# Row 4's x by the crossbar, chunk 2 and 3 re-stepped, and dilated v loaded without unread keys

## The chip, the core and the metric

The kernel runs on one core of a Trainium2 chip. The metric is the device time of one execution in microseconds. Three runs of the kernel before gave 302.06, 304.31 and 308.46 us, a median of 304.31 us.

The engines are named as the profile names them: PE (TensorE, with PEld for its weight loads), DVE (VectorE), ACT (ScalarE), POOL (GpSimd) and SP (SyncE, which here only issues DMAs). All transfers of the core go through 16 DMA engines.

## What is computed

Attention over 8 batch rows of 576 tokens and 8 heads of 64, followed by a feed-forward layer with squared ReLU on the 4608 tokens. Heads 0 to 3 use a sliding window of 32 keys, heads 4 to 7 a dilated window: 32 keys at a distance of 4.

```python
rel = pos[:, None] - pos[None, :]
mask_plain = (rel >= 0) & (rel < window)                                   # window = 32
mask_dil = (rel >= 0) & (rel < window * dilation) & (rel % dilation == 0)  # dilation = 4
attn = softmax(where(mask, q @ k.T / 8, -1e9))
x = (attn @ v), heads side by side        # (4608, 512)
h = x @ w_in                              # w_in (512, 2048)
out = relu(h) ** 2 @ w_out                # w_out (2048, 512), out (4608, 512) float32
```

## The kernel before

**Two loops laid over each other.** The attention works by batch row (0 to 7, 576 tokens each), the feed-forward layer by chunk (0 to 8, 512 tokens each). While PE does chunk c of the feed-forward layer, the attention of row c + 1 is woven in. The feed-forward work is a generator (`moe_gen` for chunks 1 and 2, `moe_seven_gen` from chunk 3 on) that yields every two to four matmuls. One yield is a step. `run` (L760) takes plans such as "34:d0 36:d1" and, at the step given, issues that part of the attention. The order of everything is thereby written out by hand: `PLANS` (L979) holds for each chunk the parts of its own row and of the row after.

**Parts of a row.** `z0`, `z1` are the dilated scores with exponential and mask (L619, L586, L590), `s0`, `s1` the sliding ones (L605). `d0`, `d1` are the products with the values for the first half of the dilated queries (tile t = 0), `e0`, `e1` for the second half (t = 1) (L680). `a0`, `a1`, `a2` are those of the sliding heads (L658). Each ends in `normalize` on DVE (L643, L644), which writes x in half precision with tokens on partitions. The feed-forward layer needs x transposed, in `xT`.

**Two ways to transpose x.** For rows under `CROSS` (5) the parts `x0`, `x1`, `y0`, `y1` do it on PE (L701, L719) with a copy by ACT (L707, L725). For rows from `CROSS` on, the `a`, `d` and `e` parts issue DMA transposes through the crossbar on SP's queue instead (L670, six per row; L689, four per row), and `w0`, `w1` (`place_dilated`, L732) put the dilated part in its place by ACT copies. Chunk c needs the first tokens of row c + 1 in `xT` when it starts.

**Accumulators.** Parts take pairs of PSUM banks in turn from a ring of two (`pair`), so that a part waits until the pair two before it has been read.

**Values.** v comes from HBM in float32 by SP's queue. `load_dilated_v` (L164) has two loads: for t = 0 72 keys (L169, 288 KB), for t = 1 128 keys (L167, 512 KB), each key with 4 heads of 1 KB. They go into `sd`, of which there is one. POOL casts `sd` to half precision (`cast_dilated_v`, L211) before `d` and `e` can run. `sd` can be loaded again when its casts are done. For the sliding heads `load_sliding_v` (L159) has six loads per row.

**SP's queue.** SP issues in the order of the program and waits in that order. In chunk 3 it goes: outputs of chunk 2 (L331), crossbar transposes of row 5's dilated k and q (L256), its sliding k and q to HBM (L244) and back through the crossbar (L252), row 5's `sd` (L169, L167), row 5's `sv` (L159), outputs of chunk 3 (L440). From chunk 4 on the ten crossbar transposes of x (L689, L670) stand between `sd` and `sv`: the code adds `load_sliding_v` for the next row at step 38 where the present row is at `CROSS` or above.

Of the kernel before, what the change touches and what calls it, by code (L numbers as in the profile page):

```python
# [13 lines left out]
P = 128  # L14
# [3 lines left out]
def kernel(  # L18
# [9 lines left out]
    nc = tc.nc  # L28

    B, H, S, D = q.shape  # L30
    W = 32
# [17 lines left out]
    CL = S // DIL  # L49
    QD = CL // 2  # L50
    PADD = P - QD
# [68 lines left out]
    sd = stg.tile([P, 2, HH, DIL * D], FP32, name="sd")  # L120
# [18 lines left out]
    def load_dilated_qk(b, m):  # L139
        for i, s in ((1, k), (0, q)):  # L140
            nc.gpsimd.dma_start(
                out=m[64 * i : 64 * (i + 1), :],
                in_=s[b, HH:H].rearrange("h (p j) d -> (h p) (j d)", j=36),
            )
# [19 lines left out]
    def load_dilated_v(b, t):  # L164
        vv = v[b, HH:H].rearrange("h (i c) d -> i h (c d)", c=DIL)
        if t:
            nc.sync.dma_start(out=sd[:, 1, :, :], in_=vv[QD - PADD : CL])  # L167
        else:
            nc.sync.dma_start(out=sd[PADD:P, 0, :, :], in_=vv[0:QD])  # L169

    def load_v(b, dilated_first=False):
        if not dilated_first:
            load_sliding_v(b)
        for t in range(2):
            load_dilated_v(b, t)
        if dilated_first:
            load_sliding_v(b)
# [350 lines left out]

    CROSS = 5

    def pt(wide):
        return pair(FP16)[:, 0, :] if wide else bank(FP16)
# [104 lines left out]
    def normalize(b, what, pav, w, n=2):  # L639
        x = xp.tile([QB, 2, HH, D], FP16, name=f"x{b}_{what}", tag="x")  # L640
        rcp = xp.tile([QB, 2, HH], FP32, name=f"rcp{b}_{what}", tag="rcp")
        pv = pav[0:w, 0:n, 0 : HH * (D + 2)].rearrange("p i (h d) -> p i h d", d=D + 2)
        nc.vector.reciprocal(rcp[0:w, 0:n], pv[:, :, :, D])  # L643
        nc.vector.tensor_tensor(  # L644
            out=x[0:w, 0:n],
            in0=pv[:, :, :, 0:D],
            in1=rcp[0:w, 0:n].unsqueeze(3).to_broadcast([w, n, HH, D]),
            op=ALU.mult,
        )
        return x  # L650

    def av_sliding(b, xs, *ms):

        pav = pair()
        for i, m in enumerate(ms):
            for h in range(HH):
                off = (h % 2) * 288 + (m % 3) * QB
                nc.tensor.matmul(  # L658
                    pav[:, i, h * (D + 2) : h * (D + 2) + D + 1],
                    AT[:, 2 * (h // 2) + m // 3, off : off + P],  # L660
                    vp[b % 2][:, m, h, 0 : D + 1],
                    start=True,
                    stop=True,
                )
        x = normalize(b, f"p{ms[0]}", pav, QB, len(ms))
        for i, m in enumerate(ms):
            if b < CROSS:
                xs[m] = x[:, i]
            else:
                nc.sync.dma_start_transpose(  # L670
                    out=xT[b % 3][:, 0:2, QB * m : QB * (m + 1)],
                    in_=x[:, i].rearrange("p h d -> p (h d)"),
                )

    def av_dilated(b, t, a):
        pav = pair()
        for e in range(2):
            for h in range(HH):
                off = e * 288 + h * QD
                nc.tensor.matmul(  # L680
                    pav[:, e, h * (D + 2) : h * (D + 2) + D + 1],
                    AT[:, 4 + 2 * a + t, off : off + P],
                    vd[b % 2][:, t, 2 * a + e, h, 0 : D + 1],
                    start=True,
                    stop=True,
                )
        x = normalize(b, f"d{t}_{a}", pav, QD if b < CROSS else QX)
        if b >= CROSS:
            nc.sync.dma_start_transpose(  # L689
                out=xd[:, t, 2 * a : 2 * a + 2].rearrange("p e c q -> p (e c) q"),  # L690
                in_=x[0:QX].rearrange("p e h d -> p (e h d)"),
            )
        return x

    def x_sliding(b, half, xs, wide):
        px = pt(wide)
        for m3 in range(3):
            m = 3 * half + m3
            x = xs[m].rearrange("p h d -> p (h d)")
            for c in range(2):  # L700
                nc.tensor.transpose(  # L701
                    px[:, 288 * c + QB * m3 : 288 * c + QB * (m3 + 1)],
                    x[:, P * c : P * (c + 1)],
                    ident[0:QB, 0:QB],
                )
        t0 = 288 * half
        nc.scalar.copy(  # L707
            xT[b % 3][:, 0:2, t0 : t0 + 288],
            px[:, 0:UW].rearrange("x (c t) -> x c t", c=2),
        )  # L710

    def x_dilated(b, t, xs, wide):
        py = pt(wide)
        for a in range(2):
            for e in range(2):
                x = xs[a][:, e].rearrange("p h d -> p (h d)")
                for c in range(2):
                    o = 288 * c + QD * (2 * a + e)
                    nc.tensor.transpose(  # L719
                        py[:, o : o + QD],  # L720
                        x[0:QD, P * c : P * (c + 1)],
                        ident[0:QD, 0:QD],
                    )
        t0 = 288 * t
        nc.scalar.copy(  # L725
            xT[b % 3][:, 2:4, t0 : t0 + 288].rearrange("x c (i r) -> x c i r", r=DIL),
            py[:, 0:UW].rearrange("x (c r i) -> x c i r", c=2, r=DIL),
        )
# [8 lines left out]
    def row_parts(b, wide):  # L737
# [9 lines left out]
            "a2": lambda: av_sliding(b, xs, 4, 5),  # L747
            "x0": lambda: b < CROSS and x_sliding(b, 0, xs, wide),
            "x1": lambda: b < CROSS and x_sliding(b, 1, xs, wide),
            "d0": lambda: ys.append(av_dilated(b, 0, 0)),  # L750
            "d1": lambda: ys.append(av_dilated(b, 0, 1)),
            "e0": lambda: zs.append(av_dilated(b, 1, 0)),
            "e1": lambda: zs.append(av_dilated(b, 1, 1)),
            "y0": lambda: b < CROSS and x_dilated(b, 0, ys, wide),
            "y1": lambda: b < CROSS and x_dilated(b, 1, zs, wide),
# [24 lines left out]
    reli = const.tile([P, QB], I16, name="reli")  # L780
    load_dilated_qk(0, nd0)
    nc.vector.memset(sd[0:64, 0, :, :], 0.0)
    nc.vector.memset(sv[0:PADP, 0, :, :], 0.0)
    nc.gpsimd.iota(reli, pattern=[[1, QB]], base=0, channel_multiplier=-1)
    make_identity(nc, ident)
    load_sliding_qk(0, ns0[0], 0)
    nc.gpsimd.memset(sd[64:65, 0, 0, 0:1], 0.0)
    load_sliding_qk(0, ns0[1], 1)
    load_dilated_v(0, 0)
    load_sliding_v(0, 0, 4)  # L790
    load_dilated_v(0, 1)
    load_sliding_v(0, 4, 6)

# [128 lines left out]
    for i, src in ((1, k), (0, q)):  # L922
        nc.gpsimd.dma_start(
            out=ns1[64 * i : 64 * (i + 1)],
            in_=src[1, 0:HH].rearrange("h (p j) d -> p h (j d)", j=9),
# [42 lines left out]
    for leaves in kept[:2]:  # L968
# [7 lines left out]
    SOON = "{}:z0 {}:z1 {}:s0 {}:s1"  # L976
    EARLY = "{}:d0 {}:d1 {}:e0 {}:y0 {}:e1 {}:a0 {}:y1 {}:a1 {}:a2 {}:x0 {}:x1"
# [1 line left out]
    PLANS = {  # L979
        1: (SOON.format(*range(24, 40, 4)) + " " + EARLY.format(*range(40, 62, 2)), ""),  # L980
        2: (
            SOON.format(18, 22, 26, 30) + " " + EARLY.format(34, 36, 38, 40, 41, 43, 45, 49, 51, 54, 59),
            SOON.format(49, 54, 60, 63),
        ),
        3: (
            EARLY.format(8, 11, 14, 17, 19, 22, 24, 27, 30, 33, 36),
            SOON.format(40, 45, 50, 55),
        ),
        4: (LATER[0] + " 57:w0 60:w1", LATER[1]),
        5: (LATER[0] + " 57:w0 60:w1", LATER[1]),  # L990
# [71 lines left out]
```

## Time and profile before

| | |
|---|---|
| three runs | 302.06, 304.31, 308.46 us, median 304.31 |
| the profiled execution | 300.74 us, span of its instructions 298.8 us |
| granted TensorE clock | 1.000 |
| PE busy | 289.2 us, 97% of the span |
| DVE, ACT, POOL busy | 203.7, 164.2, 67.6 us |
| DMA traffic | 84145 packets, 48.62 MB; HBM 189 GB/s over the span |
| SP's DMA queue (q1) | 76720 packets, 34.39 MB, 52.6% of 16 engines' span |
| POOL's DMA queue (q0) | 7248 packets, 13.63 MB, 26.0% |

Busy time is the time in which an engine had an instruction in work. The share of a DMA queue is the time that its packets took, summed over the 16 DMA engines and divided by 16 spans. SP itself has no busy time: its lines in a timeline are the stretches in which it was issuing a transfer. Such a line begins when SP reaches the instruction, and its length includes waiting for a semaphore or for room in the queue.

### The profile page before, as it was taken

The numbers are of one execution on the slowest core, as the hardware profiler recorded it, in microseconds if no ns is written. First come the engines' busy times: TensorE is split into PE (matmuls) and PEld (weight loads), VectorE is DVE, ScalarE is ACT, GpSimd is POOL, SyncE is SP. The second block draws the span as 40 slices with busy tenths as digits, with TensorE's granted clock in tenths as the row PEclk, the third lists the DMA queues.
The fourth block names the chain that finished last, engine by engine and source line by source line (L and its number), as shares of the span: only waits on it lengthen the run. The fifth ranks groups of instructions, "written<-read, shape, count | busy, mean of one in ns | idle before, by whom it ended". The sixth has DMA issues, their size and how long they took to land.

```text
span 298.8 us, 7670 instructions
## 1 busy us (share of the span) xinstructions
PE 289.2 (97%) x3152; PEld 218.5 (73%) x3152; DVE 203.7 (68%) x378; ACT 164.2 (55%) x280; POOL 67.6 (23%) x113
## 2 busy tenths in 40 slices
PE   3999999999999998999999999999999999999995
PEld 2779855555557755699889988998888876785584
DVE  7686645587723573389798979896979744853674
ACT  1768754778446954766435636563656326405610
POOL 5490017004505112620721350202230000000000
PEclk9999999999999999999999999999999999999999
DMA  6999999699999999998999998989274230022013
GB/s 115 236 209 214 211 218 223 141 186 238 172 288 199 230 208 162 236 257 189 222 241 241 166 201 81 245 186 190 40 207 99 64 107 0 2 70 70 2 35 105
DMA packets 84145, 48.62 MB, mean 163 GB/s; under 512 B 62672, under 2 KB 80336, under 8 KB 83920
## 3 DMA queue, kind: packets, MB, share of 16 engines
q1 hardware_dynamic: 76720, 34.39, 52.6%
q0 software_dynamic: 7248, 13.63, 26.0%
q8 instruction: 24, 0.39, 0.5%
q10 hardware_dynamic: 144, 0.13, 0.1%
q14 instruction: 9, 0.07, 0.1%
HBM read 39.85 MB, written 16.52 MB: 189 GB/s over the span
## 4 chain that ended last, share of the span: by engine, by line
PE 78%; DMA 13%; POOL 3%; DVE 2%; SPq 2%; issue 1%; ACT 0%; POOLq 0%; DVEq 0%
PE PS L266 37%; PE PS L410 24%; PE PS L307 10%; DMA nd<-in_k_dram 5%; DMA sd<-in_v_dram 3%; DMA n<-in_q_dram 3%; DMA sv<-in_v_dram 2%; PE PS L680 2%; PE PS L658 2%; PE PS L619 1%; SPq L159 1%; PE PS L605 1%; PE PS L719 1%; DVE S L396 1%; PE PS L701 1%
## 5 line engine op out<-in xcount | busy, mean ns | idle before, releaser
L266 PE MATMUL PS<-xT,wi 128*128 128x288 f16 (+8 forms) x1024 | 133.6, 286 | 0.0
L275 ACT ACTIVATE rt<-PS 128x512 f16<-128x512 f32 (+2 forms) x160 | 88.7, 555 | 62.0 <-PE PS L266 58.7
L266 PEld LDWEIGHTS <-wi 128*128 128x128 f16 x1024 | 97.4, 114 | 25.9
L300 DVE TENSOR_TENSOR g<-rt 128x1024 f16<-128x1024 f16 (+1 forms) x64 | 44.1, 690 | 33.2 <-ACT rt L275 33.0
L586 ACT ACTIVATE AT<-PS 128x576 f16<-128x576 f32 x64 | 38.5, 650 | 22.9 <-PE PS L605 14.7
L307 PE MATMUL PS<-wo,g 128*128 128x512 f16 x192 | 49.3, 379 | 0.0
L410 PEld LDWEIGHTS <-S 128*128 128x128 f16 x384 | 37.0, 98 | 4.6
L211 POOL CAST vd<-sd 128x512 f16<-128x512 f32 x32 | 25.0, 812 | 43.6 <-DMA sd<-in_v_dram 28.6
L410 PE MATMUL PS<-T,S 128*128 128x256 f16 x288 | 34.1, 273 | 0.0
L410 PEld LDWEIGHTS <-g 128*128 128x128 f16 x288 | 27.5, 98 | 4.0 <-issue 0.2
L207 POOL CAST vp<-sv 128x512 f16<-128x512 f32 x24 | 16.7, 702 | 55.4 <-DMA sv<-in_v_dram 53.2
L307 PEld LDWEIGHTS <-g 128*128 128x128 f16 x192 | 15.6, 98 | 12.6
L410 PE MATMUL PS<-wo,g 128*128 128x256 f16 x192 | 23.4, 273 | 0.0
L644 DVE TENSOR_TENSOR x_d<-PS,rcp_d 72x512 f16<-72x512 f32 (+1 forms) x32 | 22.0, 687 | 1.1
L590 DVE TENSOR_TENSOR AT<-AT,maskd 128x1152 f16<-128x1152 f16 x14 | 12.2, 873 | 14.2 <-ACT AT L586 14.1
L590 DVE TENSOR_TENSOR AT<-AT,maskp 128x1152 f16<-128x1152 f16 x14 | 11.0, 787 | 10.8 <-ACT AT L586 10.8
L644 DVE TENSOR_TENSOR x_p<-PS,rcp_p 96x512 f16<-96x512 f32 (+1 forms) x25 | 16.6, 665 | 0.9
L680 PEld LDWEIGHTS <-AT 128*128 128x128 f16 x256 | 11.9, 100 | 4.7 <-DVE x_d L644 1.1
L680 PE MATMUL PS<-vd,AT 128*128 128x65 f16 x256 | 13.8, 197 | 0.3 <-DVE x_d L644 0.2
L289 DVE TENSOR_TENSOR g<-rt 128x288 f16<-128x288 f16 x32 | 9.8, 307 | 5.5 <-ACT rt L275 5.3
L410 PE MATMUL PS<-T,g 128*128 128x256 f16 x96 | 12.0, 273 | 0.1
L410 PE MATMUL PS<-wo,S 128*128 128x256 f16 x96 | 11.5, 273 | 0.0
(89 smaller groups left out, 246.6 us busy)
## 6 DMA issues: line engine op xcount, KB each, us to landing
out_dram<-c SPq DMA_DIRECT2D x23, 256.0 KB, 2.2
sv<-in_v_dram SPq DMA_DIRECT2D x40, 128.0 KB, 5.7
sd<-in_v_dram SPq DMA_DIRECT2D x8, 512.0 KB, 6.1
dp<-o SPq DMA_DIRECT2D x12, 288.0 KB, 4.0
out_dram<-ot SPq DMA_DIRECT2D x11, 256.0 KB, 8.2
sd<-in_v_dram SPq DMA_DIRECT2D x8, 288.0 KB
wo<-in_moe_w_out_dram POOLq DMA_DIRECT2D x4, 512.0 KB, 14.3
n<-in_k_dram POOLq DMA_DIRECT2D x6, 288.0 KB, 7.3
```

The costliest lines, as they stand in the source:

```text
L207: nc.gpsimd.tensor_copy(vp[b % 2][:, m : m + 2, :, 0:D], sv[:, m : m + 2, :, :])
L211: nc.gpsimd.tensor_copy(vd[b % 2][:, t, c : c + 2, :, 0:D], sd[:, t, :, D * c : D * (c + 2)].rearrange("p h (c d) -> p c h d", d=D),)
L266: nc.tensor.matmul(ph[:, a - t0 : b - t0], w_in_of(dmk, ffc), xT[r % 3][:, dmk, a - r * S : b - r * S], start=(dmk == 0 and a == t0), stop ...
L275: nc.scalar.activation(rt, ph[:, 0:w], ACTF.Relu)
L289: nc.vector.tensor_mul(g[:, f2 + i, t0 : t0 + HALF], r, r)
L300: nc.vector.tensor_mul(g[:, f2 : f2 + 2, o:TOKC], rt[:, :, o:TOKC], rt[:, :, o:TOKC])
L307: nc.tensor.matmul(po, g[:, ffc, o + t * P : o + (t + 1) * P], w_out_of(ffc), start=(ffc == 0), stop=(ffc == NFF - 1),)
L410: nc.tensor.matmul(po[t], lhs(j)[:, t * P : (t + 1) * P], rhs(j), start=j == 0, stop=j == HF - 1)
L586: nc.scalar.activation(AT[:, u + i, 0:UW], ps[:, :, 0 : UW // 2], ACTF.Exp, scale=scale)
L590: nc.vector.tensor_mul(AT[:, u : u + n, 0:UW], AT[:, u : u + n, 0:UW], mask.unsqueeze(1).to_broadcast([P, n, UW]),)
L644: nc.vector.tensor_tensor(out=x[0:w, 0:n], in0=pv[:, :, :, 0:D], in1=rcp[0:w, 0:n].unsqueeze(3).to_broadcast([w, n, HH, D]), op=ALU.mult,)
L680: nc.tensor.matmul(pav[:, e, h * (D + 2) : h * (D + 2) + D + 1], AT[:, 4 + 2 * a + t, off : off + P], vd[b % 2][:, t, 2 * a + e, h, 0 : D ...
```

## The change

Four edits:

1. `CROSS` goes from 5 to 4. Row 4's x is transposed by ten DMA transposes on SP's queue, not by 28 transposes on PE and four copies on ACT. `w0` and `w1` are added to chunk 3 at steps 57 and 60. By the same constant, the `sv` loads of row 5 move from step 6 of chunk 3 to step 38, behind the crossbar transposes.
2. The plan of chunk 2: row 4's `z0`, `z1` move from steps 49 and 54 to 43 and 48, and row 3's `e1` to `x1` parts are spread differently around them.
3. Row 4's `s0`, `s1` move from steps 60 and 63 of chunk 2 to steps 2 and 5 of chunk 3. Row 5's `z0` to `s1` in chunk 3 move from 40, 45, 50, 55 to 43, 48, 53, 58.
4. The t = 1 load of dilated v, in all eight rows, leaves out the keys 16 to 40, which no query of that half reaches: it has 103 keys in place of 128 and starts at partition 25. A memset of 32 partitions on DVE at the start of the kernel keeps the partitions that are no longer loaded at zero.

```diff
     def load_dilated_v(b, t):
         vv = v[b, HH:H].rearrange("h (i c) d -> i h (c d)", c=DIL)
         if t:
-            nc.sync.dma_start(out=sd[:, 1, :, :], in_=vv[QD - PADD : CL])
+
+            k0 = QD - W + 1
+            nc.sync.dma_start(out=sd[k0 - (QD - PADD) : P, 1, :, :], in_=vv[k0:CL])
         else:
             nc.sync.dma_start(out=sd[PADD:P, 0, :, :], in_=vv[0:QD])
...
-    CROSS = 5
+    CROSS = 4
...
     nc.vector.memset(sd[0:64, 0, :, :], 0.0)
+    nc.vector.memset(sd[0:32, 1, :, :], 0.0)
...
         2: (
-            SOON.format(18, 22, 26, 30) + " " + EARLY.format(34, 36, 38, 40, 41, 43, 45, 49, 51, 54, 59),
-            SOON.format(49, 54, 60, 63),
+            SOON.format(18, 22, 26, 30) + " " + EARLY.format(34, 36, 38, 40, 41, 45, 46, 50, 52, 53, 56),
+            "43:z0 48:z1",
         ),
         3: (
-            EARLY.format(8, 11, 14, 17, 19, 22, 24, 27, 30, 33, 36),
-            SOON.format(40, 45, 50, 55),
+            "2:s0 5:s1 " + EARLY.format(8, 11, 14, 17, 19, 22, 24, 27, 30, 33, 36) + " 57:w0 60:w1",
+            SOON.format(43, 48, 53, 58),
         ),
```

`EARLY` names the steps of d0, d1, e0, y0, e1, a0, y1, a1, a2, x0, x1, and `SOON` those of z0, z1, s0, s1. Here QD = 72, PADD = 56, W = 32, P = 128 and CL = 144, so that k0 = 41 and the load writes partitions 25 to 127.

## The prediction

> **What bounds the kernel now.** I read the page first, then the chain of waits, then the timelines of SP's queue and of the first 24 us, and last the trace's records of semaphores and DMA packets.
>
> ```profile
> span 298.8 us, 7670 instructions
> ...
> PE 289.2 (97%) x3152; PEld 218.5 (73%) x3152; DVE 203.7 (68%) x378; ACT 164.2 (55%) x280; POOL 67.6 (23%) x113
> ...
> q1 hardware_dynamic: 76720, 34.39, 52.6%
> ...
> sd<-in_v_dram SPq DMA_DIRECT2D x8, 512.0 KB, 6.1
> ...
> sd<-in_v_dram SPq DMA_DIRECT2D x8, 288.0 KB
> ```
>
> PE has work nearly all the time, at a granted clock of 1.000, so work taken off PE shortens the kernel as long as nothing arrives late. The last two lines are the two loads of dilated v. The 512 KB one (128 partitions, t = 1) lands 6.1 us after its issue. The 288 KB one (72 partitions) shows no landing, since the page gives one only where all 16 DMA engines report. The semaphore records tell why: every 72-partition load gets one increment at its issue and twelve with its data, while loads of 64, 96 and 128 partitions get sixteen with their data. So 72 partitions run on 12 DMA engines.
>
> From 58 us to the end the chain of waits is almost all PE. One exception is in chunk 2 (start, length, what):
>
> ```profile
> 113.98 0.27 PE PS L658 x8
> ...
> 114.51 0.70 DVE x_p L644
> ...
> 115.25 0.31 PE PS L619 x8
> ```
>
> Row 4's `z0` needs the pair of banks that `a1` has just filled, and PE stands 1.0 us from 114.25 to 115.25. The start shows how tight the values are (start, length, engine; the bracket is idle time before):
>
> ```profile
> 8.02 3.07 SPq L167 DMA_DIRECT2D sd<-in_v_dram  x1
> ...
> 16.00 1.17 POOL L211 CAST vd<-sd 128x512 f16<-128x512 f32 x2 [0.27 <-DMA sd<-in_v_dram]
> ...
> 17.26 0.43 PE L680 MATMUL PS<-vd,AT 128*128 128x65 f16 x8
> ```
>
> The t = 1 load lands at 15.95, POOL casts at 16.00, and PE uses the result in `e0` at 17.26. Then SP's queue in chunks 3 and 4:
>
> ```profile
> 141.74 0.50 SPq L169 DMA_DIRECT2D sd<-in_v_dram  x1
> 142.33 0.42 SPq L167 DMA_DIRECT2D sd<-in_v_dram  x1
> 142.84 10.06 SPq L159 DMA_DIRECT2D sv<-in_v_dram  x6
> 153.00 4.42 SPq L440 DMA_DIRECT2D out_dram<-c  x4
> ...
> 168.91 5.55 SPq L689 DMA_TRANSPOSE xd<-x_d  x4
> 174.56 10.23 SPq L670 DMA_TRANSPOSE xT<-x_p  x6
> 184.89 3.25 SPq L159 DMA_DIRECT2D sv<-in_v_dram  x6
> ```
>
> SP has hardly a free moment. The 10.06 us for six issues are SP held back by a full queue: counting packets issued against packets done, 120 to 180 were outstanding on each engine. An issue that would go beyond about 150 waits.
>
> **The small edits.** Crossbar for row 4: 28 PE transposes leave the path, in four groups of 0.26 us (132.51, 136.34, 141.05, 142.62 in the chain): -1.05 us. ACT gives up four copies of 0.65 us for two of 1.19, off the path. SP gets ten transposes, 5.1 + 8.1 us as in its quietest stretch, with 2432 packets of 256 B. They lie between row 5's `sd` and `sv`, so `sv` and all behind them slip by some 5 us. Chunk 4 would start on the third L670, about when it lands: 0 to 2.5 us of waiting, I take 0.5, and for the starts of chunks 5 and 6 another 2 us (0 to 7). The spread in chunk 2 takes away the stall of 1.0 and makes smaller ones (`a1` behind an exponential, `x0` behind `a1`'s 0.9 us of DVE): -0.4 (-1.0 to 0). The moved `s0`, `s1` are the same 0.72 us of PE in another chunk, with 0.2 us for a pair still being read. The memset takes 0.91 us of DVE (as L782), of which 0.6 fall into idle time before L800, and the rest into PE's wait for k and q at 5.50 and 6.92: nothing. 25 x 4 packets fewer per row at 59 ns over 16 engines save 0.37 us of DMA time, and at 54 us, where DVE waits for row 2's k and q, some 0.4 us. Sum: -1.05 - 0.4 + 0.2 - 0.4 + 2.5 = about +0.8 us.
>
> **The large edit: 103 partitions.** The number of engines that a load runs on is in the rows above 12 for 72 partitions and 16 for 64, 96 and 128: each time the largest number up to 16 that divides the partitions. 103 is prime. By this row the new load runs on one engine, with 412 packets of 1 KB in one ring in place of 32 in each. The trace shows no such load, so I bound it. At the good end, the shares need not be equal and the load lands as today or 0.4 us earlier. At the bad end all 412 are on one engine, at 36 ns (46 divided by the 1.26 packets in flight in the quiet window at 202 to 209 us), 46 ns (the median packet there) or 59 ns (the mean of all 1 KB packets of this queue) each: 14.8, 19.0 or 24.3 us. I take one engine, because an equal-share split fits all four sizes seen, and 46 ns: the landing moves out by (412 - 32) x 0.046 = 17.5 us.
>
> The Trainium skill, "DMA: Bandwidth & Descriptors", section "Why a DMA increments its semaphore by 16 and not by 1", states this rule: the split takes the largest count up to 16 that divides the slowest dimension of both sides, and it names 127 partitions as an example for one. Its "Specifications" give about 27 GiB/s per engine, by which 412 KB would take an estimated 14.6 us, the good one of my three rates. By the rule the sum is the one below; without it, the +0.8 above.
>
> **What waits.** The later transfers of SP have a share on that same engine, in order, so they land behind the 412. And SP is held: with about 100 packets already out, it can go on when all but 150 are done, (412 + 100 - 150) x 0.046 = 16.7 us, as against 0.4 now. I follow each row, with today's times shifted by what has accumulated (C):
>
> - Row 0: lands at 15.95 + 17.5 = 33.45, first cast 0.6, `e0` at 34.1 in place of 17.26. +16.8. POOL stands at the cast, and so do w_in, w_out and row 1's loads behind it.
> - Row 1: lands at 51.35 + 16.8 + 17.5 = 85.7, with the cast 86.3; `e0` today 53.84, with C 70.6. +15.7.
> - Row 2: SP free at 77, then L244 to L252 as today (8.2 us), t = 1 issued at 86.9 when the casts of row 1 are done, landed 5.7 + 17.5 later, cast at 110.8. `e0` 77.81 + 32.5 = 110.3. +0.5.
> - Row 3: SP free at 104. `sv`, outputs, L244, L256, L252 take 19 us, so issue at 123, cast done 147.7; `e0` 107.78 + 33 = 140.8. +6.9.
> - Row 4: SP free at 140, issue at 159, cast done 183.3; `e0` 130.78 - 1.2 + 39.9 = 169.5. +13.8.
> - Chunk 4's start: SP free at 176; `sv` 3.3, outputs 2, L256 3, L244 with landing 4.1, L252 2.8, so row 5's load at 192.5. Free at 209.6, four L689 (5.1), three L670 (4.1) and 2.4 to land: 221.2. PE would be there at 207. +14.2.
> - Chunk 5's start: the same circle, now with 7.4 us for `sv` and the other L670: row 6's load at 240, SP free at 257.4, first two L670 landed at 267.6. PE 221.2 + 29.9 = 251.1. +16.5.
> - Chunk 6's start: row 7's load at 288, x landed at 315.3. PE 297.6. +17.7. After it no such load comes, and the last 84 us are as today.
>
> Sum 102.1 us. The +0.8 shrinks to about -1.6, since the SP delays in it are contained in these: +100 us on the profiled 300.74, so 401 us. The profile stands 3.6 us under the median of the runs shown (304.31), so I say 404 us. With 36 ns per packet each of the eight stages is about 4 us shorter: 372. With 59 it is about 5 longer: 446.
>
> **Rivals.**
>
> 1. *The load is spread anyway.* If shares may be unequal, or the load is split by another dimension, it lands in 6 us. Row 0's slack is 1.2 us, so it decides from 412 / (32 + 1.2/0.046) = 7 engines on. Against it stands that 72 partitions ran on exactly 12. Then only the small edits count: 304.3 + 0.8 = 305 us, within 2% of before. This is the case that is not slower. Chance 0.06.
> 2. *One engine, but SP is not held.* Were the ring deeper than the 150 or so that the trace shows, SP would go on issuing while it drains, and the stages of rows 3 and 4 and of the starts of chunks 5 and 6 would lose most of their 16.7 us, since the circle would fit in 30 us. Some 70 us stay: 375. Against it: the 10.06 us above, and 4.56 us for one issue at 122.64. Chance 0.13.
> 3. *One engine, and the drain is shared.* POOL's loads of the next row (n and dd) have packets on that engine too, 5.6 + 3.8 us per row by the packet records. Were they all in the drain of rows 2 to 7: +56 us, 457. In most rows they start only after L252 has landed, which is just then. Chance 0.07.
>
> **How the numbers follow.** The forecast has 0.74, its rivals the rest. Two per cent, 6 us, is about what a measurement of this kernel can tell from no change. Only rival 1 can lie within it: 0.06, and I leave 0.01 for faster; slower has 0.93. The range takes in the two rates and most of rivals 2 and 3: 365 to 450.
>
> **What would show it.** In the profile after, t = 1 loads have no landing on the page, and one data increment each; SP is held 10 us or more at or just behind each; POOL's casts wait for `sd` some 15 us a row, over 100 us in all, against 28.6 today; PE stands 10 us and more at `e0` of rows 0, 1 and 4 and at the starts of chunks 4, 5 and 6; DMA shares fall in those stretches to a tenth. If t = 1 loads land in about 6 us on all engines, the forecast is wrong at its root. If they take 20 us and the time is still under 365, SP's hold was the wrong term.

## The result, and the profile after

The changed kernel takes 442.0 us, the median of six runs (438.85 to 446.68), against 303.34 us before in as many. The ratio is 1.460, with a 95% interval of 1.449 to 1.471. The profiled execution took 444.64 us, its span is 442.9. Medians here and below are over all runs, while a ratio and its interval leave out runs that lay over 1.5% above the fastest of their kernel.

The page of the changed kernel, in the lines that answer to those of before (its lines are two or three further down in the source: L169 is the t = 1 load, L171 that for t = 0):

```profile
span 442.9 us, 7636 instructions
...
PE 307.6 (69%) x3124; PEld 226.7 (51%) x3124; DVE 203.5 (46%) x379; ACT 164.1 (37%) x278; POOL 63.8 (14%) x113
...
PEclk9855999659959986995699569975699669999999
...
sd<-in_v_dram SPq DMA_DIRECT2D x8, 412.0 KB
```

PE was 97% busy and is 69% busy. DVE, ACT and POOL are busy as long as before or less, so most of the added time is waiting. PE's own busy time rose by 18.4 us, with 28 matmuls fewer. The 412 KB load is now a line without a landing, as the 288 KB one was: not all 16 engines report. In the semaphore records each of the eight loads has one increment at its issue and one with its data, 21.4 to 29.9 us after the issue (mean 26.9). The row PEclk, all nines before, now has fives and sixes.

The list of waits of the changed kernel (engine and line, what it waited for: us in total, times, longest):

```profile
POOL vd L213 <- DMA sd<-in_v_dram: 184.1, 13, 23.4
...
PE PS L682 <- POOL vd L213: 73.0, 5, 21.4
PE PS L268 <- DMA xT<-x_p: 53.5, 3, 21.1
```

POOL waited 28.6 us for `sd` before, and 184.1 now. Eight waits of PE make up 126.5 us: five at `e0` of rows 0 to 4, where the cast values are missing, and three at the starts of chunks 4, 5 and 6, where x is missing. The first of them in the timeline (start, length, engine, and the idle time before in brackets):

```profile
37.96 1.18 POOL L213 CAST vd<-sd 128x512 f16<-128x512 f32 x2 [21.98 <-DMA sd<-in_v_dram]
38.63 0.60 PE L682 MATMUL PS<-vd,AT 128*128 128x65 f16 x8 [21.39 <-POOL vd L213]
```

These were at 16.00 and 17.26. And SP's queue in chunk 3:

```profile
224.67 0.26 SPq L169 DMA_DIRECT2D sd<-in_v_dram  x1
225.03 27.60 SPq L691 DMA_TRANSPOSE xd<-x_d  x4
252.73 7.61 SPq L672 DMA_TRANSPOSE xT<-x_p  x6
260.43 4.29 SPq L159 DMA_DIRECT2D sv<-in_v_dram  x6
```

The load itself is issued in 0.26 us. The first of the four transposes behind it then takes 23.72 us to be issued, the other three 1.2 each. SP goes on only when most of the 412 packets are through.

### The profile page after: what moved, and what is told of

It is laid out like the page before. It is cut to its first block, busy times and chain, and to the rows that moved or that the text cites. A ratio compares the mean times of both kernels' runs of the same rounds, so it can differ in the third digit from the quotient of the medians.

```text
span 442.9 us, 7636 instructions
## 1 busy us (share of the span) xinstructions
PE 307.6 (69%) x3124; PEld 226.7 (51%) x3124; DVE 203.5 (46%) x379; ACT 164.1 (37%) x278; POOL 63.8 (14%) x113
## 4 chain that ended last, share of the span: by engine, by line
PE 40%; DMA 32%; SPq 16%; issue 6%; POOL 3%; DVE 1%; ACT 1%; POOLq 0%; DVEq 0%; ACTq 0%
DMA sd<-in_v_dram 20%; PE PS L268 20%; PE PS L412 14%; SPq L691 10%; DMA nd<-in_k_dram 3%; PE PS L309 3%; DMA n<-in_q_dram 2%; SPq L246 2%; SPq L258 2%; DMA sv<-in_v_dram 2%; DMA xT<-x_p 2%; PE PS L682 2%; DMA QKTp<-dp 2%; DMA nd<-in_q_dram 1%; SPq L672 1%
## 5 line engine op out<-in xcount | busy, mean ns | idle before, releaser
L268 PE MATMUL PS<-xT,wi 128*128 128x288 f16 (+8 forms) x1024 | 144.1, 300 | 53.5 <-DMA xT<-x_p 53.5
L268 PEld LDWEIGHTS <-wi 128*128 128x128 f16 x1024 | 101.1, 117 | 84.8 <-DMA xT<-x_p 33.4
L682 PE MATMUL PS<-vd,AT 128*128 128x65 f16 x256 | 16.8, 219 | 73.0 <-POOL vd L213 73.0
L645 DVE RECIPROCAL rcp_d<-PS 72x8 f32<-72x8 f32 (+1 forms) x32 | 6.4, 200 | 112.8 <-PE PS L682 112.6
L682 PEld LDWEIGHTS <-AT 128*128 128x128 f16 x256 | 15.1, 116 | 79.4 <-issue 73.0
L309 PE MATMUL PS<-wo,g 128*128 128x512 f16 x192 | 54.8, 412 | 0.0
L213 POOL CAST vd<-sd 128x512 f16<-128x512 f32 x32 | 21.1, 688 | 186.1 <-DMA sd<-in_v_dram 184.1
L588 ACT ACTIVATE AT<-PS 128x576 f16<-128x576 f32 x64 | 38.4, 650 | 23.5 <-PE PS L607 12.5
L412 PEld LDWEIGHTS <-g 128*128 128x128 f16 x288 | 27.6, 98 | 3.8
L734 ACT COPY xT<-xd 128x576 f16<-128x576 f16 x8 | 9.0, 1166 | 52.2 <-DMA xd<-x_d 52.2
L309 PEld LDWEIGHTS <-g 128*128 128x128 f16 x192 | 16.8, 104 | 14.3 <-issue 3.3
L319 ACT COPY ot<-PS 128x512 f32<-128x512 f32 x12 | 7.0, 586 | 42.4 <-PE PS L309 35.2
```

Source lines behind the costliest of these rows:

```text
L213: nc.gpsimd.tensor_copy(vd[b % 2][:, t, c : c + 2, :, 0:D], sd[:, t, :, D * c : D * (c + 2)].rearrange("p h (c d) -> p c h d", d=D),)
L268: nc.tensor.matmul(ph[:, a - t0 : b - t0], w_in_of(dmk, ffc), xT[r % 3][:, dmk, a - r * S : b - r * S], start=(dmk == 0 and a == t0), stop ...
L309: nc.tensor.matmul(po, g[:, ffc, o + t * P : o + (t + 1) * P], w_out_of(ffc), start=(ffc == 0), stop=(ffc == NFF - 1),)
L412: nc.tensor.matmul(po[t], lhs(j)[:, t * P : (t + 1) * P], rhs(j), start=j == 0, stop=j == HF - 1)
L588: nc.scalar.activation(AT[:, u + i, 0:UW], ps[:, :, 0 : UW // 2], ACTF.Exp, scale=scale)
L682: nc.tensor.matmul(pav[:, e, h * (D + 2) : h * (D + 2) + D + 1], AT[:, 4 + 2 * a + t, off : off + P], vd[b % 2][:, t, 2 * a + e, h, 0 : D ...
```

## The experiments

The theory: the number of DMA engines that a load runs on is the largest number up to 16 that divides its partitions, so 103 run on one, and everything else in the change is worth a per cent or two. The first rival: the ten further crossbar transposes overload SP's queue.

**One edit alone, and the others without it.** `e1_only103` is the kernel before with edit 4. `e2_rows112` is the changed kernel with 112 keys:

```diff
-            k0 = QD - W + 1
+            k0 = CL - 112
```

`e3_edits123` is the changed kernel with the load of before (128 keys, no memset). `e4_before112` is the kernel before with the 112-key load and the memset. What was expected:

> The kernel before with the 103-key load and its memset alone; x of row 4 stays on PE and the plans stay. One-engine theory: each t = 1 load has one data increment some 22 to 30 us after its issue, the stalls at e0 of rows 0 to 4 come as in the changed kernel (21 + 19 + 8 + 13 + 20 = 81 us), and the starts of chunks 5 and 6 wait for x; 415 to 440 us. Rival, that the ten further crossbar transposes overload SP's queue: without them about 303 us.

> The changed kernel with one number different: the t = 1 load takes 112 keys (7 x 16) in place of 103. One-engine theory: all 16 engines take part, the load lands in about 6 us, no half-clock stretch in PE, 300 to 306 us, ratio to before 0.99 to 1.01. Crossbar rival: about 440 us as the changed kernel, since SP's queue holds the same transfers.

> The changed kernel without the fourth edit: 128 keys loaded, no memset. One-engine theory with the small edits as predicted (-1.05 PE transposes, -0.4 chunk 2, +0.2 pair, +2.5 SP): 0 to 2 us over before, ratio 1.000 to 1.008; if SP's delay stays hidden, about 0.995. Crossbar rival: about 440 us.

> The kernel before with a t = 1 load of 112 keys and the memset: 64 packets of 1 KB fewer per row, 0.24 us of 16 engines each. One-engine theory: 16 engines, lands in about 6 us, 0 to 0.5 us faster than before, ratio 0.997 to 1.001. A theory that any load that starts inside the partitions is slow: well over 320 us.

Measured, with the kernel before at 306.41 us on that chip: 432.9 us for `e1_only103` (one run); 319.0 for `e2_rows112`, ratio 1.041 (1.032 to 1.049); 316.8 for `e3_edits123`, 1.036 (1.030 to 1.043); a ratio of 1.004 (0.999 to 1.010) for `e4_before112`, which cannot be told from none.

Edit 4 alone gives 126 of the 139 us, and 112 keys in place of 103, at the same edits otherwise, bring it from 46% down to 4%. The rival falls as the cause of the 140 us. But two expectations missed: edits 1 to 3 were to cost 0 to 2 us and cost 10, and the 112-key version was to cost nothing and cost 13. The profile of `e3_edits123` shows where. SP's queue in chunk 3:

```profile
145.30 5.41 SPq L690 DMA_TRANSPOSE xd<-x_d  x4
150.80 12.30 SPq L671 DMA_TRANSPOSE xT<-x_p  x6
163.20 3.25 SPq L159 DMA_DIRECT2D sv<-in_v_dram  x6
```

and its chain of waits at the start of chunk 4 (start, length, what):

```profile
156.66 4.65 DMA xT<-x_p
...
161.45 1.66 PE PS L267 x7
```

The six transposes took 12.30 us to issue, and the third landed 4.65 us after SP had reached it. The DMA share is 1.25 from 144 to 156 us, where it was 0.39 in the kernel before from 223 to 237, the stretch from which the prediction took its 13.2 us. PE stands from 156.1 to 161.5, and again from 193.8 to 198.5 at the start of chunk 5. Then its matmuls run at half the rate: 7 in 1.66 us, where chunk 4 of the kernel before began with 8 in 0.87:

```profile
155.24 0.87 PE PS L266 x8
```

**Which of edits 1 to 3 costs the 10 us.** `e23_plans` keeps both new plans and leaves `CROSS` at 5. Against `e3_edits123`:

```diff
-    CROSS = 4
+    CROSS = 5
...
-            "2:s0 5:s1 " + EARLY.format(8, 11, 14, 17, 19, 22, 24, 27, 30, 33, 36) + " 57:w0 60:w1",
+            "2:s0 5:s1 " + EARLY.format(8, 11, 14, 17, 19, 22, 24, 27, 30, 33, 36),
             SOON.format(43, 48, 53, 58),
```

> The kernel before with both new plans (chunk 2's spread, row 4's s0, s1 in chunk 3, row 5's scores later) and CROSS left at 5: edits 1 to 3 without the crossbar edit. If the 3.6% that edits 1 to 3 cost come from the ten crossbar transposes ahead of sv on SP's queue: 303 to 308 us, ratio 0.99 to 1.01, and no wait for x of more than 3 us at the starts of chunks 4 and 5. If they come from the moved scores: 313 to 318 us, ratio about 1.03.

304.68 us, against 307.5 before on that chip: ratio 0.988 (0.982 to 0.995). The wait for x is nearly gone from its list of waits:

```profile
PEld L267 <- DMA xT<-x_p: 1.3, 2, 0.8
```

So the crossbar edit costs the 10 us, and more: from a ratio of 0.988 to one of 1.036 it is nearly 5%. The two plans without it are faster than the kernel before by 0.5 to 1.8%, by three runs against seven. It is the one version here that beats both kernels. `plan2` is the kernel before with the spread of chunk 2, without the moved `s0`, `s1` and without the later scores of row 5:

```diff
-            SOON.format(18, 22, 26, 30) + " " + EARLY.format(34, 36, 38, 40, 41, 43, 45, 49, 51, 54, 59),
-            SOON.format(49, 54, 60, 63),
+            SOON.format(18, 22, 26, 30) + " " + EARLY.format(34, 36, 38, 40, 41, 45, 46, 50, 52, 53, 56),
+            SOON.format(43, 48, 60, 63),
```

> The kernel before with the spread of chunk 2 alone: row 4's z0, z1 at steps 43 and 48 and row 3's parts as in the change; CROSS, s0 and s1 of row 4 and the loads stay as before. The 1.0 us wait of PE for row 3's a1 goes, and up to 0.6 us of smaller ones come: 0.4 to 1.0 us faster, ratio 0.997 to 0.999, within what five rounds can tell from none.

Ratio 0.998 (0.993 to 1.002) over five rounds: not to be told from none, as expected. The wait of 1.0 us at row 4's `z0` is gone from its timeline, as from that of `e23_plans`. But its profiled run lost 2.5 us at the start of chunk 5, where x came late, which the profile of the kernel before does not show. What the moved scores add to make some 1% was not taken apart.

**The load by itself.** `lone` issues the load in seven widths on an empty queue, each awaited before the next:

> No attention and no feed-forward: nine loads of dilated v alone on SP's queue, one after the other, of 128, 103, 104, 106, 112, 116, 72, 103 and 128 keys, each awaited by a DVE copy of one column; then the tile is written out, so the output is not the reference's. One-engine theory, with 4 packets of 46 ns per key shared by 16, 1, 8, 2, 16, 4, 12, 1, 16 engines and about 2 us of latency: 3.5, 21.0, 4.4, 11.8, 3.3, 7.3, 3.1, 21.0, 3.5 us from issue to landing. If shares were near equal over 13 to 16 engines: 3 to 4 us for all.

DVE's timeline, where the bracket is the wait from one copy to the next, that is, one load. Down the rows the keys are 128, 103, 104, 106, 112, 116, 72:

```profile
6.05 0.15 DVE L63 COPY seen<-sd 128x1 f32<-128x1 f32 x1 [4.10 <-DMA sd<-in_v_dram]
25.74 0.15 DVE L65 COPY seen<-sd 128x1 f32<-128x1 f32 x1 [19.53 <-DMA sd<-in_v_dram]
30.42 0.15 DVE L67 COPY seen<-sd 128x1 f32<-128x1 f32 x1 [4.53 <-DMA sd<-in_v_dram]
41.83 0.15 DVE L69 COPY seen<-sd 128x1 f32<-128x1 f32 x1 [11.25 <-DMA sd<-in_v_dram]
45.79 0.15 DVE L71 COPY seen<-sd 128x1 f32<-128x1 f32 x1 [3.81 <-DMA sd<-in_v_dram]
53.16 0.15 DVE L73 COPY seen<-sd 128x1 f32<-128x1 f32 x1 [7.22 <-DMA sd<-in_v_dram]
56.71 0.15 DVE L75 COPY seen<-sd 128x1 f32<-128x1 f32 x1 [3.40 <-DMA sd<-in_v_dram]
```

One key more, 104 instead of 103, and the load takes 4.5 us instead of 19.5. The data increments number 16, 1, 13, 2, 16, 4 and 12, in each case the largest divisor up to 16. The expectations had eight engines for 104 keys (8 x 13); 13 divides it too, and the trace shows 13. The packets of the 103-key load ran from 0.93 to 19.17 us after the issue: 18.2 us for 412, 44 ns each.

**The same widths in the whole kernel.** `k106`, `k116` and `k104` are the changed kernel with 2, 4 and, in place of the 8 expected, 13 engines on the load:

```diff
-            k0 = QD - W + 1
+            k0 = CL - 106        # 116, 104
```

> The changed kernel with 106 keys in the t = 1 load (2 x 53): two engines by the divisor pattern, 212 packets on each. Between 317 us (edits 1 to 3 alone, 32 packets) and 442 (412 packets) by a straight line: 376 us; less if the slack of some rows takes part: 365 to 380. Two data increments per load. If 106 counted as nearly 16 engines: 317.

> The changed kernel with 116 keys (4 x 29): four engines, 116 packets on each; by the straight line 345 us, with slack 330 to 345. It loads more bytes than the changed kernel, so a theory that goes by bytes would put it above 442.

> The changed kernel with one key more, 104 (8 x 13): eight engines, 52 packets on each; by the straight line 324 us, with slack 317 to 324. A theory that goes by the place at which the load starts, or by bytes, would leave it at 442.

371.9, 353.4 and 324.9 us, one run each, with before at 308.6. The time goes with the packets on the busiest engine (412, 212 and 116 give 442, 372 and 353 us; with 32 or fewer it is 317 to 325) and not with the bytes: 116 keys are more bytes than 103 and 89 us faster. `k116` missed its range by 8 us. `k104` lies within 1 us of a range that was worked out from eight engines and 52 packets. With its 13 engines it has 32 packets on each, as `e3_edits123` has, and was 8 us slower in its one run, on another chip. The runs of `e2_rows112` alone reach from 315.8 to 323.0, so this does not tell 13 engines from 16.

**Another queue.** `pool103` lets POOL issue the load:

```diff
-            nc.sync.dma_start(out=sd[k0 - (QD - PADD) : P, 1, :, :], in_=vv[k0:CL])
+            nc.gpsimd.dma_start(out=sd[k0 - (QD - PADD) : P, 1, :, :], in_=vv[k0:CL])
```

> The changed kernel with the 103-key load issued by POOL instead of SP; nothing else moves. Theory A, the split over engines is SP's way of dividing and POOL divides otherwise: landings of some 6 to 10 us, 315 to 325 us as with edits 1 to 3 alone. Theory B, any queue puts 103 keys on one engine: SP is no longer held behind the load, but the casts still wait 20 us and more: 385 to 430 us.

440.2 us. In its DMA view all engines report now, but no sooner:

```profile
sd<-in_v_dram POOLq DMA_DIRECT2D x8, 412.0 KB, 28.7
```

In the three rows where the increments can best be told apart, 15 come 10 to 15 us after the issue and the sixteenth at 29 to 30. The packets say the same in seven of the eight loads: 103 packets of 4 KB, about one at a time over 21 to 23 us, beside 15 x 103 packets of 16 B. So POOL's queue, too, puts the data on one engine. Theory B holds, but the time is above its range. SP is no longer held behind the load, yet its 16-engine transposes still wait for the one engine. PE now stands mostly at scores, behind transposes of q and k that have a share on that engine:

```profile
PE PS L607 <- DMA QKTp<-dp: 40.1, 3, 16.1
...
PE PS L621 <- DMA QKTd<-dd: 26.9, 3, 14.1
```

**Another place in the queue.** `late103` moves the loads of rows 5 to 7 behind the crossbar transposes:

```diff
                 turn(b, n, dd)
                 load_dilated_v(b, 0)
-                load_dilated_v(b, 1)
+                if b <= CROSS:
+                    load_dilated_v(b, 1)
...
+            if b >= CROSS:
+                more.append((37, lambda b=b + 1: load_dilated_v(b, 1)))
```

> The changed kernel with the 103-key loads of rows 5 to 7 moved behind the ten crossbar transposes in SP's queue (step 37). Theory A, order: only what stands behind the load in the queue suffers, so the waits for x at the starts of chunks 4 to 6 (19.7 + 21.4 + 13.2 us) shrink to those of edits 1 to 3 (about 5 each) and the time falls to 400 to 410 us. Theory B, a drain of 20 us and more per row is on the path wherever it stands: the waits move to e0 of rows 5 to 7, and the time stays at 430 to 450 us.

446.05 us. The waits at the starts of chunks 4 to 6 are gone, and `e0` has them all, in all eight rows:

```profile
PE PS L682 <- POOL vd L213: 130.3, 8, 20.0
```

A drain of over 20 us per row is on the path at either place, as theory B says. The loads of rows 5 and 6, which POOL's loads of the next row now no longer accompany, landed in 21.4 and 21.2 us here, against 28.8 and 28.9 in the changed kernel.

## Why the prediction was right, by its steps

**The large edit** was right in its mechanism, from the row that it rested on: twelve data increments for 72 partitions. One engine was shown by the increments of the changed kernel, by `lone`, and by 112 keys undoing the loss. The rule in the Trainium skill ("DMA: Bandwidth & Descriptors", "Why a DMA increments its semaphore by 16 and not by 1") holds for all seven widths of `lone`. The 27 GiB/s per engine of the same page's "Specifications" would make an estimated 14.6 us for the load; measured were 18.2, and that decides.

**The size** was short. The 442.0 us lie inside the stated 365 to 450, but near the upper end, which stood there for packets of 59 ns and for rival 3. The packets took 44 ns in `lone`; a part of rival 3 and the half clock, which is in no term, brought the time there. That it stayed inside the range is in part luck. (By its own terms the end for 59 ns is eight times 5 on 404, which is 444 and not 446.) Of the signs, one did not come: the DMA share in the eight waits was 0.20 to 0.87 and not a tenth. The eight steps, predicted and measured, as what each adds to the shift against the profile of before:

| | predicted | measured |
|---|---|---|
| `e0` of row 0 | 16.8 | 21.4 |
| row 1 | 15.7 | 19.0 |
| row 2 | 0.5 | 8.2 |
| row 3 | 6.9 | 12.5 |
| row 4 | 13.8 | 20.1 |
| start of chunk 4 | 14.2 | 21.3 |
| start of chunk 5 | 16.5 | 23.5 |
| start of chunk 6 | 17.7 | 15.6 |
| from there to the end | 0 | 2.5 |
| sum | 102.1 | 144.1 |

The predicted steps are all waits. Measured, PE waited 126.5 us in these eight places, 24.4 more, and the other 17.6 us of the shift are slower work. Three terms were short or left out.

*The landing.* The sum had 6.1 + 17.5 = 23.6 us in the middle rows, and the mean was 26.9. It counts by itself at `e0` of rows 0, 1, 3 and 4. The 46 ns were right (`lone`: 44). What was missing is company on that engine. Rows 2 and 7 landed in 22.1 and 21.4 us, the other six in 27.3 to 29.9. Row 7 has no next row to load, and row 2's load was already through (120.7) when POOL issued the next row's n at 123.45. In rows 1 and 3 to 6 POOL issued n and dd within 5 us of the load, and in row 0 the loads of w_in ran beside it. That is rival 3, which was given 0.07: its mechanism holds in part, with some 7 us in a row and not 9.4. `late103` shows it, where rows 5 and 6 without this company landed 7 to 8 us sooner.

*The half clock.* The slower work was left out of the prediction. The busy time of each engine from 292 to 311 and from 311 to 316 us in the changed kernel (the length; PE, PEld, DVE, ACT, POOL; then the granted clock, DMA share, GB/s):

```profile
292.00:311.00 19.00, 0.00 (x0) 0.11 (x1) 0.00 (x0) 2.02 (x2) 1.18 (x2) 0.52 0.40 40
311.00:316.00 5.00, 4.96 (x36) 3.76 (x36) 1.43 (x3) 1.39 (x3) 0.00 (x0) 0.50 0.20 39
```

PE stops at 289.9, the clock falls to a half at 292.9, and PE's first 5 us of new work run at 0.50. By the clock record, each of the eight waits is followed by 4.1 to 6.1 us of work at half clock, 40.5 us in all, so about 20 us of loss. That fits the 17.6, from which the 1 to 2 us saved by edits 1 and 2 are already taken. In the traces of all these kernels, every gap of PE from 2.5 us up that began at full clock has a half-clock record behind it, and none of up to 2.1 us has. The Trainium skill, "TensorE: Matmul & The Clock Gate", section "Part 1: The HAM clock gate (the "warmup" mystery)", says that full clock returns after a busy window of about 3.4 us; here 4.1 to 6.1 us of work passed first.

*SP's hold* was put at 16.7 us and was 23.7 in chunk 3 and 23.9 in chunk 4: a transpose was issued only when about 5 us of the drain were left (248.74 against the landing at 253.5), that is an estimated 100 packets and not 150. In the kernel before, counted at the end of each issue, plain loads had, by an estimate from the trace, up to some 145 packets outstanding on each engine and crossbar transposes up to some 105; the 150 held for plain loads alone. In chunk 5, without POOL's loads in the drain, the hold was 16.1, and the start of chunk 6 is the one step that was put too high. Row 2's step is the hold as well: behind row 1's load SP was free at 87.5 and not at 77, so row 2's load was issued at 98.6 and not at 86.9.

**Rival 2**, an unheld SP, was not what happened: SP was held. `pool103` takes the hold away and is no faster, though it also puts POOL's own loads behind the drain.

**The small edits** were put at +0.8 us, and edits 1 to 3 cost 10. The step that failed is the wait for row 4's and row 5's x, at the starts of chunks 4 and 5 (chunk 4 has the tokens 2048 to 2559 and row 4 begins at 2304, so a chunk c needs row c's first tokens, not row c + 1's): 0.5 us for the one and 2 for chunks 5 and 6 together in the sum, 5.4 and 4.8 measured in `e3_edits123`, each with half-clock work after it. The transposes were taken at the 13.2 us of the quietest stretch and needed 17.9 at that point of the kernel, where the DMA engines are full. The bounds given there were 0 to 2.5 us for the first wait, which it left, and 0 to 7 for the others, which held. The PE time that was to be saved is there: 3124 matmuls in place of 3152, and no wait at row 4's `z0` in `e23_plans` and `plan2`. But these 1 to 2 us are less than one such wait.

## What to carry to other kernels

Count the DMA engines of each transfer before counting its bytes: trimming 25 of 128 keys cut 20% of the bytes and took the load from 16 engines to one, while 112 keys keep all 16 and 104 keep 13. A load that ends late costs PE twice, once as a wait and, where the wait was 2.5 us or longer, once as some 5 us at half clock after it. Moving work from the busiest engine to an in-order queue that is itself full (here 1 us of PE to 13 to 18 us of SP) needs a look at the first thing that stands behind it.

## What was not expected of the hardware

POOL's queue divided the 103 keys no better than SP's: the last of its 16 increments came at 28.7 us in the median. And SP was let go 5.7 to 6.8 us before the landing of the 103-key load where a plain transfer stood behind it (rows 0 to 4), but only 4.7 to 4.9 us before it where a crossbar transpose did (rows 5 to 7).
